# Single-token decode attention on one core: a key and value ring of three 64 KB slots in place of four of 32 KB, with one TensorE loop over key units

## The chip, the core and the metric

The kernel runs on one core of one Trainium2 chip. The metric is the device time in microseconds (us). A run whose time agrees with the fastest of its kernel within 1.5% is called fast. Times of a trace are counted from the start of its span; the span is some 2 us shorter than the device time.

## The reference, cut to what matters

```python
x = A_x                                   # one token, D = 448
xn = layernorm(x)
# A: attention of one query over a long cache. 16 query heads, 8 key/value heads, 65536 positions, head size 256, bf16
q = (xn @ wq).reshape(1, 1, 16, 256)      # two query heads share a key/value head
p = softmax(q . k_cache / 16)             # k_cache: [1, 8, 65536, 256], 268 MB
a = (p @ v_cache) @ wo                    # v_cache: 268 MB
# B: one token through a gated FFN (448 -> 1792 -> 448), gated by sigmoid(xn @ w_r)
b = xn + (silu(xn @ w_gate) * (xn @ w_up)) @ w_down * sigmoid(xn @ w_r)
out = x + a + b
```

The work per byte is small: 549 MB must be read once, nearly all of it keys and values.

## The kernel before: the parts that the change and the argument touch

The cache of a head is cut into four units (U = 4) of 16384 positions, 128 per partition: a unit is 64 KB per partition, 8 MB in all, for keys and again for values. There are 32 key units (k0 to k31) and 32 value units (v0 to v31). The value unit of turn t belongs to the head of the key units four turns earlier, since the maximum over a head's scores must be known first; so v0 can be used only after k3.

```python
NKT = 8            # buffers for transposed keys: two sets of four
NSLOT = 4          # ring slots
CH = 64            # positions per partition and slot: 32 KB
SLOT = CH * Dh
ring   = S_("ring", [P, NSLOT * SLOT], BF16)     # 128 KB per partition
w_area = S_("w_area", [P, WQN], BF16)            # wq, later gate and up weights
# ... (wd_a, wo_cur, wo_end: 6 + 3.5 + 3.5 KB for other weights)

# the load queue, in order (SyncE waits for FREE of the slot before it issues)
item("wq", ...)
for u in range(U):
    for c in range(HC):
        slot_item("k", u, c)                     # 32 KB per partition
    if u == U // 2 - 1:
        item("wg", ...); item("wd", ...)         # FFN weights, 4.7 MB, early
for t in range(NT):                              # NT = 28 turns
    slot_item("k", t + U, 0)
    pair_item(t)                                 # both halves of a value unit: one 64 KB descriptor per partition
    # ... (wo of a head every fourth turn)
    slot_item("k", t + U, 1)
# ... (the last head's four value units)
```

TensorE transposes keys in sets of 16 positions per partition (four groups of four, `k_T`), VectorE copies groups 0 to 2 from PSUM and ScalarE group 3 (`EV`), TensorE multiplies the set with the query (`k_QK`, into ps_q), ScalarE copies that (`EVQ`), and TensorE spreads it over partitions (`k_JT`, into ps_s). A unit has eight sets. The value product is `pe_V`: 32 matmuls for each half of a unit.

```python
    W(e, "T", s, m)
    W(e, "QK", s - 2)          # a copy of set s may run before the scores of set s-1
# ...
def turn_B(t):                 # one turn: key unit t+4 and value unit t
    u = t + U
    k_slots(sets_of(u, 0), s0, at)     # four sets
    pe_V(t, 0, True, True); pe_tot(t); pe_V(t, 1, True, True)
    dve_ob(t)
    k_slots(sets_of(u, 1), s0, at)     # four sets
    k_JT(s1 - 2); k_QK(s1 - 1); pe_attn(t); k_JT(s1 - 1)    # the drain of the unit
```

## Time and profile before

| | before |
|---|---|
| device time, median of 3 | 1280.76 us (1280.38 to 1282.76) |
| load queue's packets | 99.7% of 16 DMA engines' span |
| TensorE, VectorE, ScalarE busy | 77%, 46%, 36% |
| TensorE's waits for keys and values | 82.6 + 144.4 us |

The lines below are from the page of the kernel before. The two rows headed DMA and GB/s are the span in 40 equal slices: the busy tenths of the 16 DMA engines (9 is 90% or more) and what they moved. The line of q1 gives the load queue's packets, MB and the share of 16 engines' span that the packets took. The line that starts with a share of DMA is the chain of work that ended last, by engine.

```profile
span 1279.0 us, 23059 instructions
...
PE 984.8 (77%) x9859; PEld 674.4 (53%) x9859; DVE 584.2 (46%) x1091; ACT 459.6 (36%) x655; POOL 4.6 (0%) x35
...
DMA  9999999999999999999999999999999999999998
GB/s 409 427 426 432 434 430 422 436 427 446 430 429 430 428 446 430 435 423 428 439 438 432 430 425 436 439 435 430 424 435 430 445 430 424 432 431 442 425 437 346
...
q1 hardware_dynamic: 18322, 549.04, 99.7%
...
DMA 65%; PE 33%; issue 1%; DVE 0%; SPq 0%; ACT 0%; ACTq 0%
```

Read together: the DMA engines have no slice to spare, TensorE has a quarter of its time. The next lines are from the list of waits of the kernel before: who waited for whom, total us, number of waits, the longest.

```profile
PE ps_o L372 <- DMA ring<-in_A_v_cache_dram: 144.4, 32, 19.1
...
PE ps_t L372 <- DMA ring<-in_A_k_cache_dram: 82.6, 28, 4.9
```

In about 28 turns TensorE waits 227 us for loads, 8 us a turn. A turn's two units take 38.8 us to load, so its TensorE work is about 31 us. And here is a stretch, 140 to 165 us, in the view of DMA queues of the kernel before (40 slices of 0.6 us; a packet of 2.4 us counts in full in the slice in which it starts, so single slices jump and a share can exceed 100%):

```profile
DMA  9496969696969699999799497979494999299929
...
q1 hardware_dynamic: 270, 11.08, 102.5%
```

### The profile page before, as it was taken

The numbers are of one execution on the slowest core, as the hardware profiler recorded it, in microseconds if no ns is written. First come the engines' busy times: TensorE is split into PE (matmuls) and PEld (weight loads), VectorE is DVE, ScalarE is ACT, GpSimd is POOL, SyncE is SP. The second block draws the span as 40 slices with busy tenths as digits, with TensorE's granted clock in tenths as the row PEclk, the third lists the DMA queues.
The fourth block names the chain that finished last, engine by engine and source line by source line (L and its number), as shares of the span: only waits on it lengthen the run. The fifth ranks groups of instructions, "written<-read, shape, count | busy, mean of one in ns | idle before, by whom it ended". The sixth has DMA issues, their size and how long they took to land.

```text
span 1279.0 us, 23059 instructions
## 1 busy us (share of the span) xinstructions
PE 984.8 (77%) x9859; PEld 674.4 (53%) x9859; DVE 584.2 (46%) x1091; ACT 459.6 (36%) x655; POOL 4.6 (0%) x35
## 2 busy tenths in 40 slices
PE   4998877778777787677786777877787876888754
PEld 3877554555554564445554545644455544556421
DVE  2676544454444554344543445543355443555310
ACT  1555433353333543234432244432334333344210
POOL 1000000000000000000000000000000000000000
PEclk9998888897878998888988889988799788899885
DMA  9999999999999999999999999999999999999998
GB/s 409 427 426 432 434 430 422 436 427 446 430 429 430 428 446 430 435 423 428 439 438 432 430 425 436 439 435 430 424 435 430 445 430 424 432 431 442 425 437 346
DMA packets 18342, 549.22 MB, mean 429 GB/s; under 512 B 1942, under 2 KB 3992, under 8 KB 5144
## 3 DMA queue, kind: packets, MB, share of 16 engines
q1 hardware_dynamic: 18322, 549.04, 99.7%
q8 instruction: 8, 0.13, 0.0%
q14 instruction: 6, 0.05, 0.0%
q10 hardware_dynamic: 6, 0.00, 0.0%
HBM read 549.03 MB, written 0.00 MB: 429 GB/s over the span
## 4 chain that ended last, share of the span: by engine, by line
DMA 65%; PE 33%; issue 1%; DVE 0%; SPq 0%; ACT 0%; ACTq 0%
DMA ring<-in_A_k_cache_dram 59%; PE ps_t L372 24%; PE ps_q L372 6%; DMA ring<-in_A_v_cache_dram 5%; PE ps_m L372 2%; PE ps_s L372 1%; DMA wr_row<-in_B_w_r_dram 0%; SPq L826 0%; ACT s L450 0%; DVE rowsf L340 0%; DVE xe_row L335 0%; DVE stat L312 0%; DVE rowsf L342 0%; DVE rowsf L319 0%; ACTq L826 0%
## 5 line engine op out<-in xcount | busy, mean ns | idle before, releaser
L372 PE MATMUL ps_t<-ident_f,ring 128*128 128x128 f32 x4096 | 546.7, 288 | 103.4 <-DMA ring<-in_A_k_cache_dram 82.6
L426 DVE COPY kt_buf<-ps_t 128x1024 bf16<-128x1024 bf16 x768 | 488.1, 684 | 268.0 <-PE ps_t L372 267.5
L372 PEld LDWEIGHTS ps_t<-ident_f,ring 128*128 128x128 f32 x4096 | 474.0, 147 | 211.3 <-issue 103.2
L428 ACT ACTIVATE kt_buf<-ps_t 128x1024 bf16<-128x1024 bf16 x256 | 262.2, 1024 | 242.8 <-PE ps_t L372 242.7
L372 PE MATMUL ps_o<-ring,p_sb 128*4 128x512 bf16 x2040 | 193.1, 545 | 144.5 <-DMA ring<-in_A_v_cache_dram 144.4
L450 ACT ACTIVATE s<-ps_q 98x512 bf16<-98x512 f32 x256 | 152.9, 597 | 273.5 <-PE ps_q L372 273.5
L372 PEld LDWEIGHTS ps_o<-ring,p_sb 128*4 128x4 bf16 x2040 | 55.7, 106 | 252.2 <-issue 233.5
L372 PE MATMUL ps_q<-kt_buf,q_cur 128*2 128x512 bf16 x2048 | 164.4, 398 | 0.0
L517 ACT ACTIVATE p_sb<-S_sb 128x128 bf16<-128x128 bf16 x64 | 19.0, 309 | 252.2 <-PE ps_o L372 249.2
L532 DVE RECIPROCAL rs<-ps_m 128x4 f32<-128x4 f32 x29 | 5.3, 182 | 226.5 <-PE ps_m L372 226.5
L372 PEld LDWEIGHTS ps_s<-sel_bf,s 128*128 128x128 bf16 x1024 | 59.9, 98 | 53.8 <-ACT s L450 50.8
L372 PE MATMUL ps_s<-sel_bf,s 128*128 128x8 bf16 x1024 | 63.9, 168 | 22.6 <-ACT s L450 22.6
L568 DVE CAST ob_sb<-ps_o 100x512 bf16<-100x512 f32 x29 | 20.1, 692 | 117.2 <-PE ps_o L372 117.2
L605 DVE TENSOR_TENSOR rowsf<-ps_m,rowsf 1x448 f32<-1x448 f32 x28 | 17.1, 612 | 53.9 <-PE ps_m L372 53.9
L372 PEld LDWEIGHTS ps_m<-rowsum,ones_f 128*128 128x128 f32 x116 | 21.6, 262 | 22.3 <-issue 22.3
L372 PEld LDWEIGHTS ps_q<-kt_buf,q_cur 128*2 128x2 bf16 x2048 | 27.1, 79 | 10.2 <-issue 5.0
L372 PE MATMUL ps_m<-wo_cur,oT_sb 128*1 128x448 bf16 x112 | 25.7, 352 | 0.0
L372 PE MATMUL ps_m<-rowsum,ones_f 128*128 128x2 f32 x116 | 24.0, 312 | 0.0
L372 PE MATMUL ps_m<-xnT_sb,w_area 128*128 x112 | 14.7, 184 | 2.8 <-issue 2.8
L372 PEld LDWEIGHTS ps_m<-wo_cur,oT_sb 128*1 128x1 bf16 x112 | 9.3, 83 | 13.5 <-issue 0.9
L474 DVE CAST S_sb<-ps_s 128x256 bf16<-128x256 f32 x32 | 12.9, 404 | 4.3 <-PE ps_s L372 4.3
L372 PEld LDWEIGHTS ps_m<-xnT_sb,w_area 128*128 x112 | 11.7, 104 | 5.8 <-issue 3.3
(87 smaller groups left out, 161.7 us busy)
## 6 DMA issues: line engine op xcount, KB each, us to landing
ring<-in_A_k_cache_dram SPq DMA_DIRECT2D x64, 4096.0 KB, 26.4
ring<-in_A_v_cache_dram SPq DMA_DIRECT2D x2, 4096.0 KB, 31.1
ring<-in_A_v_cache_dram SPq DMA_DIRECT2D x2, 2048.0 KB, 28.9
w_area<-in_A_wq_dram SPq DMA_DIRECT2D x1, 3584.0 KB, 11.2
wo_cur<-in_A_wo_dram SPq DMA_DIRECT2D x7, 448.0 KB, 17.4
ring<-in_A_v_cache_dram SPq DMA_DIRECT2D x2, 1024.0 KB, 31.0
w_area<-in_B_w_gate_dram SPq DMA_DIRECT2D x1, 1568.0 KB, 24.0
w_area<-in_B_w_up_dram SPq DMA_DIRECT2D x1, 1568.0 KB, 27.4
```

The costliest lines, as they stand in the source:

```text
L372: return pe.matmul(*a, **k)
L426: O(e, ("EV", s, m), lambda it: nc.vector.tensor_copy(out=kt[:, :], in_=tb[:, :]), f"ev{m}")
L428: O(e, ("EV", s, m), lambda it: nc.scalar.activation(out=kt[:, :], in_=tb[:, :], func=ACTF.Copy), f"ev{m}")
L450: O("act", ("EVQ", s), lambda it: nc.scalar.activation(out=s2[s % 2][0:QROWS, :], in_=ps_q[0:QROWS, :], func=ACTF.Copy), "evq")
L474: O("dve", ("SCOPY", u), lambda it: nc.vector.tensor_copy(out=S, in_=ps_sn))
L517: O("act", ("PC", t, c), lambda it: nc.scalar.activation(out=p_sb[:, c, :, :], in_=S_sb[:, n:n + CH, :], func=ACTF.Copy), "pc")
L532: O("dve", ("RS", t), lambda it: nc.vector.reciprocal(out=rs[:, :, :], in_=ps_m[0:P, C_TOT:C_TOT + NH * rep]))
L568: O("dve", ("OB", t), lambda it: nc.vector.tensor_copy(out=ob_sb[0:OROWS, :], in_=ps_o[0:OROWS, :]))
L605: O("dve", ("RES", t), lambda it: nc.vector.tensor_tensor(out=base_f, in0=ps_m[0:1, C_BIG:C_BIG + D], in1=base_f, op=ALU.add))
```

## The change

Its intent: make the keys' descriptors 64 KB too, as the values' were; to make room, weights give up their own areas and live in a ring slot, wq at the start and all others at the end. TensorE's program becomes one loop over key units in which a unit's last steps run in the next unit's first sets, so that no unit is drained.

```diff
-NKT = 8
-NSLOT = 4
+NKT = 4
+NSLOT = 3
 CH = 64
-LAST = [32, 16, 8, 4, 4]
+LAST = [64, 32, 16, 8, 4, 4]
@@
-    SLOT = CH * Dh
+    SLOT = HC * CH * Dh
@@ the load queue: keys in slots 0 and 1, values in slot 2
+    def k_item(u):
+        need = [("FREE", u - 2)] if u >= 2 else ()
+        if 2 <= u < U:
+            need = {0: [("FREEH", u - 2)], 1: need}
+        slot_item("k", u, u % 2, [("slot%d" % (u % 2), CH), ("half%d" % (u % 2), CH)] if u < U else None, need)
+    def v_item(t):
+        slot_item("v", t, 2, None, [("VFREE", t - 1)] if t else [("BASECOL",), ("QT",), ("R",), ("CONST",)])
+    item("wq", [(wq_area, flat_src(A_wq, WQN), "wq")])
+    for u in range(U - 1):
+        k_item(u)
+    v_item(0)
+    k_item(U - 1)
+    k_item(U)
+    k_item(U + 1)
+    for t in range(1, NT):
+        v_item(t)
+        if t + U + 1 < NU:
+            k_item(t + U + 1)
+    # ... v28, then gate, up, down and seven heads of wo into slot 2, v29, v30, v31 in pieces
@@ a copy of set s now waits for the scores of set s-1
-        W(e, "QK", s - 2)
+        W(e, "QK", s - 1)
@@ a turn
+        for q in sets:
+            # ... wait for the unit (q == 0), for its second half (q == 4)
+            for n, m in enumerate(TORD):          # TORD = (3, 0, 1, 2)
+                k_T(s, m, ap, q * SETN)
+                if (q, n) in at:
+                    at[(q, n)]()
+                if n == 1:
+                    k_QK(s - 1)
+            k_JT(s - 2)
+        at = {(3, 0): pe_m1t, (4, 0): pe_bc, (SETS - 1, 0): pe_oT}    # each under a run-time condition
+        k_sets(u, range(0, CSETS + 1), at)        # five sets
+        pe_V(v, 0, True, True); pe_tot(v); pe_V(v, 1, True, True); dve_ob(v)    # "the value block"
+        k_sets(u, range(CSETS + 1, SETS), at)     # three sets
# ... (output projection of 28 turns gathered into one at the end; query projection unrolled; the loop code itself)
```

## The prediction

> **What bounds it now.** The DMA engines. The slices row shows them at 9 (90% or more) in 39 of 40 slices, the queue table gives the load queue 99.7% of 16 engines' span for 549 MB, and the chain of waits is 65% DMA. TensorE is busy 77%; in the list of waits it waits 82.6 us for key and 144.4 us for value loads: about 8 us of each 38.8 us turn. By the DMA packets, the queue is idle only 1.8 us at the start and 3.5 us at the end. A 64 KB packet takes 2421 ns (median), a 32 KB one 1214 ns: 433 and 432 GB/s over 16 engines. [...]
>
> **Taken away.** About 3650 pairs of 32 KB packets become 64 KB ones; by means (2 x 1216.4 against 2424.7 ns) that is 8 ns a pair, 1.9 us over 16 engines. Fewer small pieces and completion packets give an estimated 0.5 us. On the critical path: about 2.5 us, 0.2%.
> The drains between key blocks (about 3 us a turn: two 0.7 us waits for the ps_q copy, a 0.6 us loop edge, small matmuls), the 28 output projections, and the query projection's loop gaps (0.45 us x 6) go, but from TensorE, which has time to spare: no gain.
>
> **Added.** With 4 transposed-key buffers instead of 8, an eviction waits for the score matmul of the set just before. The cycle is then three VectorE copies (1.9 us), the score matmul (0.6) and two handoffs: about 2.75 us a set instead of 2.53. Branches may cost 2 to 4 us a turn (estimate from the loop edges). A turn of TensorE becomes an estimated 34 to 37 us, under the 38.8 us of its transfers, with little margin.
>
> **Where it hurts.** Values now have one slot. At steady state this is hidden: v(t+1) follows 19.4 us of keys, and v(t) is consumed about 9 us after landing. Not at the start: the queue's order there is k4, k5, v1; v1 needs v0's slot, and v0 is consumed in the middle of k4's turn. From k4's landing that takes five sets (14 to 17 us), the value block (8 us) and 1 us to issue; the only transfer meanwhile is k5 (19.4 us). I expect the queue empty for 4 to 9 us near 145 to 160 us. Keys have two slots in the first four units, where a unit of PE work (23 to 25 us) exceeds its transfer; k5 may wait another 0 to 6 us, near 125 to 133 us. The FFN weights have moved to the end, where I find no wait: projection and FFN (about 20 us) fit within two value transfers.
>
> **Sum.** 1280.8 - 2.5 + about 8 = 1286 us; 1278 to 1299 should hold it 8 times in 10. Faster by over 2%: 1%; within 2%: 90%; slower by over 2%: 9%.
>
> **What would show it.** Right: far fewer 32 KB packets, 64 KB ones still near 2421 ns; a dip in the DMA row between 120 and 165 us and nowhere else; the queue's wait at v1 ending on the value matmul. Wrong: no dip (then about 1278), or dips in every turn.
>
> **What would make it wrong.** If branches cost far more than a loop edge, or the copies' cycle is over 3 us, the turn exceeds 38.8 us, TensorE bounds the 28 turns, and each microsecond over costs 28. If sets run faster, the start's bubble vanishes.

No term of the sum is touched: 1280.8 - 2.5 + about 8 = 1286 us. In the 2.5 us, 1.9 us come from the packet times of the trace before; the 0.5 us for small pieces and completion packets is the author's estimate, and can be set against the 1941 completion packets of 4 bytes in that trace, 9 ns each, 1.1 us over 16 engines.

## The result, and the profile after

The time is 1286.50 us, median of 4 (1286.22 to 1289.65), against 1280.68 us (1280.38 to 1282.76, 4 runs) of the kernel before in the same rounds: a ratio of 1.0048, 95% interval 1.0029 to 1.0066. Ratios here and below are the mean time of one kernel's fast runs over that of the other's of the same rounds, so they are not quite the ratio of the medians quoted. By the 2% criterion it is the same; by the interval it is slower by 0.3 to 0.7%.

The same lines of the page, of the changed kernel:

```profile
span 1284.3 us, 23619 instructions
...
PE 986.9 (77%) x9791; PEld 660.5 (51%) x9791; DVE 576.1 (45%) x1079; ACT 436.1 (34%) x655; POOL 8.0 (1%) x38
...
DMA  9999899999999999999999999999999999999998
GB/s 405 412 432 438 339 443 425 425 447 433 427 429 449 429 425 447 431 429 425 449 433 425 431 447 429 425 447 433 427 425 451 431 425 435 443 429 425 411 449 354
...
q1 hardware_dynamic: 13426, 549.03, 99.2%
```

TensorE's share is the same 77%. The rate falls to 339 GB/s in the fifth slice, 128 to 160 us, and the DMA digit of that slice drops to 8; between there and the end no slice falls below 411. The view of DMA queues of the changed kernel for 140 to 165 us:

```profile
DMA  0999299929992000000000009500990099009900
...
q1 hardware_dynamic: 129, 7.41, 70.6%
```

The last packets start near 148 us and end by about 150; the next start at 155.1 us. When the next loads were issued is in the timeline of SyncE, the engine that issues them, in the changed kernel (start us, us, engine, line, operation, out<-in; the first row is k4 and k5, the second is v1, the third k6):

```profile
103.83 23.16 SPq L882 DMA_DIRECT2D ring<-in_A_k_cache_dram  x2
154.11 0.33 SPq L882 DMA_DIRECT2D ring<-in_A_v_cache_dram  x1
162.51 0.33 SPq L882 DMA_DIRECT2D ring<-in_A_k_cache_dram  x1
```

v1 is issued at 154.11 us, when v0's slot comes free. What SyncE waited for is in its list of waits in the changed kernel, 120 to 200 us; ps_o is what the value matmuls write, and the longest of these two waits, 27.1 us, is the one from the end of k5's issue (126.98 us) to 154.11:

```profile
SPq L882 <- PE ps_o L411: 45.9, 2, 27.1
```

The next lines are from the timeline of TensorE, ScalarE and SyncE in the changed kernel from 126 to 156 us, cut: k4's first sets, the exponentials and the value block of v0. In brackets is the engine's idle time just before, and what ended it.

```profile
130.50 1.97 PE L411 MATMUL ps_t<-ident_f,ring 128*128 128x128 f32 x8 [3.79 <-DMA ring<-in_A_k_cache_dram]
...
132.39 1.02 PE L411 MATMUL ps_q<-kt_all,q_cur 128*2 128x512 bf16 x8
...
133.35 1.97 PE L411 MATMUL ps_t<-ident_f,ring 128*128 128x128 f32 x8
...
136.91 0.63 PE L411 MATMUL ps_q<-kt_all,q_cur 128*2 128x512 bf16 x8
...
137.46 1.09 PE L411 MATMUL ps_t<-ident_f,ring 128*128 128x128 f32 x8
...
139.75 0.63 PE L411 MATMUL ps_q<-kt_all,q_cur 128*2 128x512 bf16 x8
...
147.71 0.85 ACT L562 ACTIVATE S_sb<-S_sb,negmax 128x512 bf16<-128x512 bf16 x1
...
149.80 1.90 PE L411 MATMUL ps_o<-ring,p_sb 128*4 128x512 bf16 x32 [2.02 <-ACT p_sb L572]
...
152.17 1.90 PE L411 MATMUL ps_o<-ring,p_sb 128*4 128x512 bf16 x32
...
154.11 0.33 SPq L882 DMA_DIRECT2D ring<-in_A_v_cache_dram  x1
```

From top to bottom: TensorE waited 3.79 us for k4, its first transposes then ran at half the speed (1.97 us for eight, later 1.09; the granted TensorE clock in the trace's records is 0.5 of full from 128.8 to 135.6 us and 1.0 from there to 193.6), the score matmuls of successive sets are 2.84 us apart (136.91, 139.75), TensorE waited 2.02 us for the probabilities, which waited for the exponentials, and then used v0 in 4.3 us. The next lines are from the list of waits of the changed kernel.

```profile
PE ps_t L411 <- DMA ring<-in_A_k_cache_dram: 136.5, 28, 6.5
...
PE ps_o L411 <- DMA ring<-in_A_v_cache_dram: 82.3, 26, 13.2
```

219 us of waits for keys and values in 28 turns, 7.8 us a turn: the steady turns are still bounded by the loads, with as much to spare as before.

Two numbers recur below. Both come from the trace's records of DMA packets, each with its start, length and size. *Packet time* is the sum of all packets' lengths over 16 engines: 1276.4 us before, 1274.9 us after. *Empty stretch* is the time from 140 to 165 us in which no packet ran, summed over the 16 engines and divided by 16, packets clipped to the window: 0.0 us before, 6.3 us after. (The share of 70.6% above says 7.4 us of 25, because it counts packets by their start.)

### The profile page after: what moved, and what is told of

Read it like the earlier page. It is cut to its first block, busy times and chain, and to the rows that moved or that the text cites. A ratio compares the mean times of both kernels' runs of the same rounds, so it can differ in the third digit from the quotient of the medians.

```text
span 1284.3 us, 23619 instructions
## 1 busy us (share of the span) xinstructions
PE 986.9 (77%) x9791; PEld 660.5 (51%) x9791; DVE 576.1 (45%) x1079; ACT 436.1 (34%) x655; POOL 8.0 (1%) x38
## 4 chain that ended last, share of the span: by engine, by line
DMA 65%; PE 24%; ACT 6%; issue 3%; SPq 2%; DVE 0%; ACTq 0%; DVEq 0%
DMA ring<-in_A_v_cache_dram 44%; DMA ring<-in_A_k_cache_dram 21%; PE ps_t L411 9%; PE ps_o L411 9%; ACT kt_all L481 5%; PE ps_q L411 4%; SPq L882 2%; PE ps_m L411 2%; DMA ring<-in_A_wo_dram 1%; ACT S_sb L562 1%; ACT p_sb L572 0%; DVE kt_all L479 0%; DVE kt_all L698 0%; ACTq L984 0%; PE ps_s L411 0%
## 5 line engine op out<-in xcount | busy, mean ns | idle before, releaser
L411 PE MATMUL ps_t<-ident_f,ring 128*128 128x128 f32 x4096 | 620.5, 296 | 167.4 <-DMA ring<-in_A_k_cache_dram 136.5
L479 DVE COPY kt_all<-ps_t 128x1024 bf16<-128x1024 bf16 x768 | 486.9, 684 | 401.4 <-PE ps_q L411 393.3
L481 ACT ACTIVATE kt_all<-ps_t 128x1024 bf16<-128x1024 bf16 x256 | 261.9, 1023 | 571.3 <-PE ps_q L411 571.2
L411 PE MATMUL ps_o<-ring,p_sb 128*4 128x512 bf16 x2044 | 160.6, 469 | 97.2 <-DMA ring<-in_A_v_cache_dram 82.3
L411 PE MATMUL ps_q<-kt_all,q_cur 128*2 128x512 bf16 x2056 | 172.6, 414 | 0.7 <-DVE kt_all L479 0.6
L411 PEld LDWEIGHTS ps_q<-kt_all,q_cur 128*2 128x2 bf16 x2056 | 26.6, 79 | 49.0 <-issue 49.0
L532 DVE TENSOR_REDUCE m1p<-S_sb (+1 forms) x33 | 13.9, 422 | 4.4
L530 DVE CAST S_sb<-ps_s 128x256 f32 (+1 forms) x33 | 13.6, 413 | 1.9 <-PE ps_s L411 1.9
L562 ACT ACTIVATE S_sb<-S_sb,negmax 128x512 bf16<-128x512 bf16 x16 | 13.2, 850 | 3.0 <-DVE negmax L556 3.0
L411 PE MATMUL ps_m<-diag,ones_f 2*128 2x2 f32 x58 | 11.0, 256 | 0.6 <-DVE diag L547 0.6
```

Of the source, the lines that this page charges most:

```text
L411: return pe.matmul(*a, **k)
L479: O(e, ("EV", s, m), lambda it: nc.vector.tensor_copy(out=kt[:, :], in_=tb[:, :]), f"ev{m}")
L481: O(e, ("EV", s, m), lambda it: nc.scalar.activation(out=kt[:, :], in_=tb[:, :], func=ACTF.Copy), f"ev{m}")
L530: O("dve", ("SCOPY", u), lambda it: nc.vector.tensor_copy(out=S_sb[:, at(it, SBN), :], in_=ps_sn), "sc")
L532: O("dve", ("SMAX", u), lambda it: nc.vector.tensor_reduce(out=m1p[:, :, at(it, 1)], in_=S_sb[:, at(it, SBN), :].rearrange("p n i -> p i n ...
L562: O("act", ("EXP", h, i), lambda it, i=i: nc.scalar.activation(out=S_sb[:, :, i], in_=S_sb[:, :, i], func=ACTF.Exp, bias=negmax[:, i:i + 1 ...
```

## The experiments

All kernels gave the right result. Theory A: the whole loss is the one empty stretch, because v1 must wait for v0's slot and v0 is used in the middle of k4's turn; against it stand about 2 us of packet time saved. Rival B: the single value slot and the four transposed-key buffers cost a little in every turn. Rival C: the weights at the end cost it. "Span" is that of the profiled execution. The ratios are to the kernel before in the same rounds, where its median was 1281.29 us for the first four experiments, 1280.63 us for the four of the rounds of "changed, again" (itself, the transpose order, halves and early, all three) and 1280.83 us for the last three; times of different rounds are not compared to better than some 2 us.

| kernel | median us (runs) | ratio to before | span | empty stretch | span less stretch | packet time |
|---|---|---|---|---|---|---|
| before | 1280.68 (4) | | 1279.0 | 0.0 | 1279.0 | 1276.4 |
| changed | 1286.50 (4) | 1.0048 | 1284.3 | 6.3 | 1278.0 | 1274.9 |
| changed, again | 1288.39 (5) | 1.0057 | 1286.5 | 9.3 | 1277.2 | 1274.2 |
| k4, k5 in halves | 1280.64 (6) | 0.9992 | 1280.2 | 3.3 | 1276.9 | 1274.0 |
| block one set later | 1288.71 (5) | 1.0054 | 1286.8 | 9.5 | 1277.4 | 1274.5 |
| the same, again | 1288.80 (5) | 1.0060 | 1286.1 | 9.3 | 1276.8 | 1273.8 |
| block two sets later | 1291.69 (5) | 1.0085 | 1288.7 | 11.5 | 1277.2 | 1274.2 |
| values in 32 KB | 1289.80 (5) | 1.0061 | 1288.0 | 8.5 | 1279.5 | 1277.2 |
| useless matmuls | 1290.43 (4) | 1.0071 | 1287.9 | 10.7 | 1277.3 | 1273.9 |
| transpose order | 1286.01 (5) | 1.0038 | 1285.2 | 8.1 | 1277.1 | 1274.1 |
| early maximum | 1285.99 (5) | 1.0044 | 1283.6 | 6.4 | 1277.2 | 1274.2 |
| halves and early | 1279.09 (5) | 0.9987 | 1277.0 | 0.3 | 1276.8 | 1274.0 |
| all three | 1278.54 (5) | 0.9982 | 1276.4 | 0.0 | 1276.4 | 1273.6 |

The column to look at is "span less stretch". For every kernel with the change's packets it lies between 1276.4 and 1278.0 us, while the stretch goes from 0 to 11.5 us.

### k4 and k5 in halves

```diff
-        if 2 <= u < U:
+        if 2 <= u < U + 2:
-        ... ("half%d" % (u % 2), CH)] if u < U else None, need)
+        ... ("half%d" % (u % 2), CH)] if u < U + 2 else None, need)
-                W_item("pe", ("k", u, 0) if q == 0 else ("k", min(u, U - 2 + u % 2), 1))
+                W_item("pe", ("k", u, 0) if q == 0 else ("k", min(u, U + u % 2), 1))
```

> The changed kernel with one edit: the fifth and sixth key units (k4, k5) are also loaded as two 32 KB halves on two semaphores, so that TensorE can start on k4 when its first half has landed. Theory A (the whole loss is the one stretch of empty load queue at 149 to 155 us, because v1 waits for v0's slot): TensorE no longer waits 3.8 us for k4 and does not fall to the slow clock after it (the first set took 5.4 us instead of 2.85, about 2.6 us), so v0 is consumed about 6.4 us sooner, the empty stretch of 6.3 us all but vanishes (under 1 us) and the time is 1280.2 us (1279.5 to 1281.5). If the slow clock plays no part, 2.5 us of the stretch stay and the time is 1282.7. Rival B (the single value slot and the four key buffers cost about 0.2 us in each of 28 turns) and rival C (the weights at the end cost it): the time stays near 1286.5.

Measured: 1280.64 us, median of 6, ratio 0.9992 (0.9980 to 1.0004). The loss is gone within the interval, which neither rival allows: this edit touches no steady turn and nothing at the end. But in the traced execution only half of the stretch is gone, 3.3 us are left, so there theory A had the size wrong. The timeline of TensorE of this kernel shows why; the two rows are the value block of v0.

```profile
143.85 3.57 PE L411 MATMUL ps_o<-ring,p_sb 128*4 128x512 bf16 x32 [2.02 <-ACT p_sb L572]
...
147.88 1.90 PE L411 MATMUL ps_o<-ring,p_sb 128*4 128x512 bf16 x32
```

TensorE does go on from k3 to k4 without a wait, and v1 is issued at 149.83 us instead of 154.11. But the 2.02 us wait for the exponentials is still there, and after it the block's first half ran at half speed, 3.57 us instead of 1.90 (the mean granted clock from 140 to 160 us is 0.91). The edit took away one idle gap and left the other. Packet time is lower too, though 512 keys' descriptors are 32 KB again, so the last microsecond of the gain may be scatter. The traced execution (1282.08 us) is one of three slower ones, 1281.40 to 1282.87 us; the other three took 1279.08 to 1279.87 us, with spans of 1277.2 to 1278.0 us. If their span less stretch is 1276.9 us too, they had 0.3 to 1.1 us of stretch, near what theory A expected; they have no trace.

### The value block one set later

```diff
-        k_sets(u, range(0, CSETS + 1), at)
+        k_sets(u, range(0, CSETS + 2), at)
-        k_sets(u, range(CSETS + 1, SETS), at)
+        k_sets(u, range(CSETS + 2, SETS), at)
```

> The changed kernel with the value block one set of keys later in each turn (after six sets, not five). Theory A: v0's slot comes free one set, 2.84 us, later, so the empty stretch grows from 6.3 to about 9.1 us and the time from 1286.5 to 1289.3; every later turn absorbs the shift (TensorE waits 7.6 us a turn for DMA). Rival B: a set more or less before the block changes nothing in the sum of a turn, 1286.5, or, if turns are tight, more than 1300. Rival C: 1286.5.

Measured: 1288.71 us, ratio 1.0054 (1.0041 to 1.0067); empty stretch 9.5 us. The stretch and the time are what was expected against the changed kernel's first trace. But the changed kernel itself, repeated below in other rounds, can have a stretch of 9.3 us, so this run alone shows no effect.

### Values in 32 KB descriptors

```diff
 def v_item(t):
-    slot_item("v", t, 2, None, [("VFREE", t - 1)] if t else [...])
+    for k, w in enumerate([[("VFREE", t - 1)] if t else [...], ()]):
+        item(("v", t, 0), [(slots[2][:, k * HALF:(k + 1) * HALF]..., rows_src("v", t, k * CH, CH), "slot2")], w)
+    fed[("v", t)] = (2, [("slot2", SBN)])
```

> The changed kernel with each value unit (but the last two kinds of pieces at the end) loaded by two DMAs of 32 KB a partition on one semaphore, waited for together: the opposite of what the change did to the keys, at nothing else. Theory A (a pair of 32 KB packets costs 8 ns more than a 64 KB one): 28 units x 128 pairs x 8 ns over 16 engines is 1.8 us more, 1288.3. Rival (the size of the descriptor is worth nothing, or the gain of the change in packet time came from elsewhere): 1286.5, within 0.5.

Measured: 1289.80 us, ratio 1.0061 (1.0048 to 1.0074), with a stretch of 8.5 us. Because the stretch scatters between runs, the time says little. The packets say it: packet time is 1277.2 us against 1273.6 to 1274.9 us of all other changed kernels, 2.3 to 3.6 us more for 3584 pairs, and span less stretch is 1279.5 against 1276.4 to 1278.0. So a 64 KB packet in place of two of 32 KB is worth a little over the 1.8 us expected here, and it is the only gain of the change that these runs show.

### Useless matmuls in front of every value block

```diff
         def block():
+            # ... wait for v(t), the probabilities and the free accumulator
+            O("pe", ("SPIN", v), lambda it: [mm(ps_o[32 * g:32 * g + 2 * rep, :], lhsT=zero_bf[:, :], rhs=slots[2][:, 0:2 * Dh],
+                                                start=True, stop=True, tile_position=(0, 32 * g), skip_group_check=True)
+                                             for _ in range(16) for g in range(NG)][-1])
             pe_V(v, 0, True, True)
```

> The changed kernel with 64 useless matmuls of 512 columns (about 3.8 us at full clock, up to 7 at half clock) in front of the value block of each of the 28 turns, after the values have landed. Theory A: steady turns have 7.6 us to spare, so only the first one shows: the empty stretch grows by 3.8 us (at most 7) and the time to about 1290.3 (1289.5 to 1294). Rival B (turns are tight): 28 x 3.8 us more, near 1390, or at least above 1300.

Measured: 1290.43 us, median of 4, ratio 1.0071 (1.0056 to 1.0085). (The 3.8 and 7 us expected of a spin are twice the 1.90 and 3.58 us that half a value block of 32 matmuls took in the changed kernel's first trace, at 149.80 and at 721.99 us.) Rival B is out: 28 turns were given extra TensorE work and the time moved by 2 to 4 us in all. Where the extra work of the other 27 turns went is in this kernel's list of waits:

```profile
PE ps_o L411 <- DMA ring<-in_A_v_cache_dram: 134.6, 31, 13.7
...
PE ps_t L411 <- DMA ring<-in_A_k_cache_dram: 34.8, 28, 6.1
```

The waits for loads fell from 219 to 169 us: the turns paid from what they had to spare. Span less stretch, 1277.3 us, stays among those of the other kernels. The 50 us are less than 28 times the spin's cost. One turn shows how: after a wait of 4.69 us for values the spin took 5.75 us, against 3.62 us in front of v0's block, and the block's two halves 1.90 us each after it, while in the changed kernel's turn at that time (718 us) the block itself took 2.75 and 3.58 us after a wait of 3.41 us. So there the spin took over the slow phase that the block had before. TensorE's busy time in the whole trace rose by only 64 us, from 986.9 to 1051.1, while the 28 spins took 157 us.

### The changed kernel again

> The changed kernel unaltered, to have its time of the same rounds as the next three: 1286.5 us (1286 to 1289), one empty stretch of 6 to 7 us near 148 to 156 us.

Measured: 1288.39 us, median of 5 (1286.11 to 1289.81), ratio 1.0057 (1.0043 to 1.0070). The stretch in its trace is 9.3 us, not 6 to 7. The three rows are the value block of v0 (matmuls of the first half, of the row sums, of the second half) in this run of the changed kernel:

```profile
148.85 2.71 PE L411 MATMUL ps_o<-ring,p_sb 128*4 128x512 bf16 x32 [2.02 <-ACT p_sb L572]
151.48 1.02 PE L411 MATMUL ps_m<-rowsum,ones_f 128*128 128x2 f32 x4
152.43 3.58 PE L411 MATMUL ps_o<-ring,p_sb 128*4 128x512 bf16 x32
```

In this execution TensorE ran the block at half speed after the same 2.02 us wait, and took 7.2 us for it instead of the 4.3 us seen at first. That is the whole difference of 3.0 us in the stretch, and the likely reason why the changed kernel's runs lie between 1286.1 and 1289.8 us.

The granted clock differs with the speed: its mean from 140 to 165 us is 0.86 in this trace and 1.00 in the first, where 32 matmuls took 1.90 us against up to 3.58 us here. The kernel with k4 and k5 in halves is like this one (2.02 us of waiting, then 3.57 us for the first half); the kernel with values in 32 KB is like the first (2.02 us, then 1.90 us for each half, and a mean clock of 1.00 from 140 to 160 us). So the length of the wait alone does not decide the speed; what does is not shown here.

### Another order of the transposes

```diff
-TORD = (3, 0, 1, 2)
+TORD = (0, 3, 1, 2)
```

> The changed kernel with the order of the four transpose groups 0, 3, 1, 2 instead of 3, 0, 1, 2. In its trace a set takes 2.84 us, and its loop runs over the ScalarE copy (1.02 us) of group 3, eight transposes (about 1.0), the score matmul (0.63) and handoffs, not over the three VectorE copies (1.89) as the prediction had it. If that reading is right, the transposes of group 0 can now start after one VectorE copy (0.69 us), and the loop falls to that of the three VectorE copies plus score matmul, about 2.65 to 2.7 us a set; v0 is consumed about 0.8 us sooner, the empty stretch shrinks by about 0.8 us and the time is about 0.8 us under that of the unaltered changed kernel. If the VectorE loop bound it already, the set stays at 2.84 us and nothing moves.

Measured: 1286.01 us, ratio 1.0038 (1.0024 to 1.0051). A set now takes 2.77 us in its trace, not the 2.65 to 2.7 expected: the VectorE loop is only 0.07 us shorter than the ScalarE loop was, since three copies (1.89 us in the changed kernel's trace) and the score matmul (0.63 us) leave 0.25 us of the 2.77 for the two handoffs, from the score matmul to the first copy and from the last copy to the next matmul. So the loop did run over ScalarE, but there was little to gain. The time is 2.4 us under the unaltered kernel of the same rounds by the medians; five sets of 0.07 us explain 0.4 us of it, and what the rest is stays open beside the scatter of the clock. The traced execution, at 1287.02 us, also ran most of its value block's first half at half speed (3.15 us).

### Halves, and the maximum earlier

```diff
-        at = {(3, 0): pe_m1t, (4, 0): pe_bc, ...
+        at = {(2, 3): pe_m1t, (3, 1): pe_bc, ...
 # and the halves of k4 and k5 as above
```

> The halves of k4 and k5, and the transposed maximum and its broadcast about half a set to a set earlier in the turn (after the third set's transposes and in the middle of the fourth's). With halves alone 3.4 us of the stretch were left, because TensorE waited 2.0 us for the exponentials in front of the value block and ran its first half at the slow clock after that (3.57 us instead of 1.90). Theory A: this wait and the slow half go, 2 to 3.7 us, and the stretch is 0 to 1.4 us; the time is 2 to 3 us under the kernel with halves alone, about 1278.5 (1277.5 to 1280), and under before by about 2 us. If the rest of the stretch has another cause, it stays near 3 us and the time near 1280.6.

Measured: 1279.09 us, ratio 0.9987 (0.9974 to 1.0001); empty stretch 0.3 us. In the trace the two halves of the block take 1.90 us each, with no wait in front. The timeline of TensorE of this kernel:

```profile
140.35 0.62 PE L411 MATMUL ps_q<-kt_all,q_cur 128*2 128x512 bf16 x8 [1.47 <-ACT s L503]
...
142.01 1.90 PE L411 MATMUL ps_o<-ring,p_sb 128*4 128x512 bf16 x32
...
144.38 1.90 PE L411 MATMUL ps_o<-ring,p_sb 128*4 128x512 bf16 x32
```

The exponentials are not free: they now hold up ScalarE one set before, and the score matmul there waits 1.47 us for its copy. But that wait does not lead to a slow block (the mean granted clock from 120 to 180 us is 1.00 in this trace), and the net is enough.

### The maximum earlier, alone

> The earlier maximum and broadcast without the halves of k4 and k5. The wait in front of the value block (2.0 us) goes, but the exponentials then hold up ScalarE in the set before (1.5 us in the kernel with both), so the net is about 0.5 us; and the block should run at full clock (4.3 us instead of 4.3 to 7.3). Empty stretch 5.5 to 6.5 us, the time near 1285.5 (1284.5 to 1286.5). If the two edits are not additive, because k4's landing no longer binds, the stretch would be under 3 us.

Its edit is the `at` line above without the halves. Measured: 1285.99 us, ratio 1.0044 (1.0030 to 1.0057), stretch 6.4 us, block at full speed (1.90 us for each half). As expected. In the traces neither edit alone empties the stretch; k4's landing and the exponentials stand one behind the other on the way to v0's slot.

### All three

> As the one before, and the transpose order 0, 3, 1, 2 as well. Theory A: no empty stretch left, 1278.3 us (1277 to 1279.5), which is the time before less the packet time that the 64 KB descriptors save (2276 would be less than any theory allows); the order adds nothing once the stretch is gone.

"The one before" is the kernel with halves and the earlier maximum, and 2276 is a slip for 1276. The edits are those of that kernel and the transpose order. Measured: 1278.54 us, median of 5 (1278.03 to 1279.61), ratio 0.9982 (0.9968 to 0.9996). No empty stretch. The gain over the kernel with halves and the earlier maximum, 0.55 us by the medians, is within the scatter. This version beats both kernels: the one before by 2.1 us by the medians, the changed one by 9.9 us. The view of DMA queues for 140 to 165 us of this kernel:

```profile
DMA  4949494969997999299949997799949994949497
...
q1 hardware_dynamic: 227, 10.94, 101.8%
```

### The value block later: reference and second step

> The value block one set later once more, as the reference for the next one: 1288.7 us, empty stretch 9.5 us. In its first run the extra set (2.84 us) hid the 2.0 us wait for the exponentials and the block ran at full clock, so that it lost nothing against the unaltered changed kernel in its slower form.

Measured: 1288.80 us, ratio 1.0060 (1.0046 to 1.0073), stretch 9.3 us. With six sets in front, the exponentials are ready and the block runs at full speed (1.90 us for each half), so the extra set replaced a wait and a slow block of about the same length.

> The value block one more set later (after seven sets). There is no wait left to hide, so theory A says one set, 2.84 us, more of empty queue than with the block after six sets: about 12.3 us, and the time up by 2.8 us, 1291.5 (1290.5 to 1292.5), while span less empty stretch stays at 1277 us as in all kernels so far that have the same packets (1276.4 to 1278.0). Rival (the second experiment's lack of an effect against the unaltered kernel means that the place of the block does not matter): 1288.7.

The edit is `CSETS + 3` in place of `CSETS + 2` in both lines. Measured: 1291.69 us, ratio 1.0085 (1.0072 to 1.0099), stretch 11.5 us. One set of 2.84 us, with nothing left to hide, costs 2.9 us by the medians of the same rounds; the stretch grew by 2.2 us, a little less than expected. The rival is out, and the place of the block in the turn sets the loss directly. The view of DMA queues for 140 to 165 us of this kernel:

```profile
DMA  9999494949400000000000000000009950099009
```

Rival C was given no experiment of its own. What speaks against it: span less stretch of the kernels with the change's packets is below the kernel before, with the weights at the end in all of them, and no empty stretch shows there. The output-projection weights' packets of 1792 bytes take 78.3 ns on average instead of 74.1 (0.5 us in the sum of 2048 packets over 16 engines), which is within the packet times above.

## Why the prediction was right, point by point

- **The time.** 1286 us was predicted, 1286.5 us measured; in a later set of rounds 1288.4 us. Both lie in the range. That the first agrees to 0.5 us is partly luck. The "about 8" of the sum stood for the empty stretch and k5's wait; the stretch was 6.3 us and k5 did not wait, while packet time fell by 1.5 us and not 2.5, and these errors offset each other in part.
- **What bounds it.** Right. The loads bound the kernel before and after. In steady turns TensorE waits 7.8 us for them, and useless work there left span less stretch where it was (1277.3 us).
- **What the 64 KB descriptors give.** Predicted 2.5 us. Packet time fell by 1.5 to 2.8 us between traces, and the same change undone on the values cost 2.3 to 3.6 us. Right in size. Of the 0.5 us estimated for small pieces nothing shows: the 4-byte completion packets fell from 1.1 to 0.8 us, but those of the output-projection weights rose by 0.5.
- **No gain from the drains.** Right. The drains are gone and TensorE's waits for loads are about as long as before, 219 against 227 us. The drains' 3 us a turn, as the prediction estimates them, went into slower sets: 2.84 us in place of 2.53, 2.5 us over the eight sets of a unit.
- **The empty queue before v1.** Right in place and reason, and about right in size: 4 to 9 us near 145 to 160 us were predicted, 6.3 and 9.3 us were found near 148 to 157 us, and the wait ended on the value matmuls. Removing the stretch by two edits removed the loss.
- **Its parts were off and cancelled.** Predicted from k4's landing: five sets 14 to 17 us, the block 8 us, 1 us to issue. In the first trace: 17.3 us of sets from the first transposes of k4 (130.49) to the last matmuls in front of the wait, a wait of 2.0 us for the exponentials, which the prediction did not have, and a block of 4.3 us at full speed (7.2 us in the other run), then 0.95 us from issue to the first packet.
- **k5's wait.** Predicted 0 to 6 us; there was none. A unit took 22.8 us (k4 was issued at 103.83 us, k5 at 126.65), just under the predicted 23 to 25, and k3 was done before k4's transfer ended.
- **A set.** Predicted 2.75 us over the VectorE copies; it is 2.84 us, over ScalarE's copy of group 3 and the two groups of transposes (eight in all) behind it. The VectorE loop is 2.77 us.
- **The branches.** Predicted 2 to 4 us a turn, and a turn of 34 to 37 us. Measured is about 31 us (38.8 less 7.8). The score matmuls are 2.84 to 2.9 us apart across the edge of a unit as well, so the branches cost TensorE nothing that can be seen. This was the term furthest off, and it fed the risk of 9% for a time over 2% longer.

## What to carry to other kernels

When the load queue is the bound, a change that enlarges the slots must be checked at each place where the queue's order meets a slot that is not free yet, above all at the start, where fewer transfers lie between a slot's use and its next load than in a steady turn. Count the transfer time queued between the two, and the consumer's time from the landing that it waits for: here 19.4 us stood against 25 in the first trace and 27 in the second. Such a gap can be closed without giving the change back, by landing the consumer's input in smaller pieces and by starting its longest dependence (here the maximum and the exponentials) earlier, and both may be needed at once: with the first alone three of six runs were still 1.5 to 4 us longer than the others, with both the five runs lie within 1.2 us.

## What the traces measured beside the change

- Eight fp32 transposes took 1.97 us after a wait of 3.79 us for loads, at a granted clock of 0.5, and 1.09 us some 7 us later, at 1.0 (changed kernel, first trace). The granted clock is 1.0 there from 53.7 to 128.8 us, where TensorE worked on key units alone, in work that is mostly transposes.
- One core loaded with 64 KB packets of 2421 ns (median), 433 GB/s over 16 engines, and with 429 GB/s over the whole span before. No run here has two cores loading at once.
- Two packets of 32 KB take 2 x 1214 ns, one of 64 KB 2421 ns by the medians of the trace before, 7 ns a pair.
- On an empty queue, the first packet of v1 came 0.95 us after the start of the issuing instruction (154.11 us) and 0.62 us after its end (changed kernel, first trace).
